# Gated mix of linear attention and a gated MLP: weight sums on another engine, the last chain's sums spread over more units

## The chip, the cores and the metric

The kernel runs on one core of one Trainium2 chip. The time is the device time of one execution in microseconds (us), the median of several executions. TensorE (PE) multiplies; VectorE (DVE), ScalarE (ACT) and GpSimd (POOL) do elementwise work; the queue of SyncE (SP) issues nearly all DMAs, in program order. Each engine works through its own instructions in order and waits on semaphores for the others.

## The reference

For x of 2048 rows and 576 columns the kernel computes, in float32:

```python
g = sigmoid((x * gate_w).sum(-1, keepdims=True))
a = linear_attention(x, wqkv) @ wo          # 32 heads of 18
h = gelu(x @ w_gate) * (x @ w_up)           # 576 -> 4608
b = h @ w_down                              # 4608 -> 576
out = g * a + (1 - g) * b
```

The change touches the MLP alone: the end of the gate and up products, and the whole of `h @ w_down`, called down here.

## The kernel before

Each float32 operand is split into a high part (rounded on ACT) and a low part (the rest, subtracted on DVE or POOL), and a product is three matmuls: high by high, high by low, low by high. Fewer products are made by fast matrix multiplication, which trades products for sums of blocks.

**Gate and up.** A list of *chains* (`CHAINS`), one per block of 256 hidden columns, half of the rows, and gate or up, each of seven products (lines 854 for the matmul). A table `plan`, filled by `put(frame, i, do)`, says what else is issued after step `i` of a frame, so it sets the order on all engines. `weight_sums` (line 373, four subtractions on POOL) prepares the block sums of the next weights. `s_make` (line 1240) makes low parts of the sums of x; for the last third of the rows of x that is on POOL. The chain ends with `extras`: sums of blocks of h that down will need (lines 996 and 999, on DVE, 128 by 512 each), which are stored to DRAM by SP (line 1008), some after loading an earlier block back (line 1014). The last chain's sums cannot be made before it ends, and are made during down, from the list `late`, whose entries `later()` takes off one by one.

**Down.** 26 products (the table `DOWN`), each of three *units* `c` = 0, 1, 2, so 78 units numbered u from 0. A unit is 36 matmuls (line 1377) in four groups of rows t, in two halves. Its operands:

- h: loaded raw from DRAM (line 1210) into one of three raw buffers (a fourth, `e123`, joins when `later()` says so), then `h_make(j)`: high part on ACT (1217 or 1220), low part on DVE (1218 for a negated one, 1221 else), 128 by 1536. There are four places for the result.
- weights: blocks of `w_down` loaded by line 1167 into tiles of 128 by 864. `weight.sums(j)` (line 1178) makes the sums of such blocks that the table names (`made`), `weight.make(j)` the high part on ACT (1183) and the low part on POOL (1184). There are fifteen tiles, and three more once `late` is empty.

At the third unit of a product the results in PSUM are added into the accumulator `acc` by DVE (line 1387, 128 by 288, with the factor 1 - g), once per group of rows and per place in the output where the product counts. Line 1383 copies a result to another set of banks where a later product starts from it. Where the next product goes on in the same banks (a `c` in the table), its first matmul must wait until DVE has read them. That holds for products 0 and 1 (units 0 to 2, then unit 3), and again for product 4, which starts at unit 12 in the banks of product 3.

The main loop of down, which sets the order on every engine:

```python
    for u in range(len(UNITS)):
        unit(u, 0)
        h_make(u + 3)
        w_make(u + 3)
        w_sums(u + 5)
        unit(u, 1)
        if u % 3 != 2:
            later()
        if u in (7, 12, 20):
            acc_load((0, 2, 3)[(7, 12, 20).index(u)])
```

`w_sums(j)` also issues the weight loads up to unit j + 3. `acc_load(i)` loads a quarter of the attention result into `acc`.

Of the kernel before, what the change touches and what calls it, by code (L numbers as in the profile page):

```python
# [114 lines left out]
def tile_gated_mix(ctx, tc, xt, xs, xn, wk, wv, wq, wo, wgu, wdn, cst, out):  # L115
    nc = tc.nc
# [247 lines left out]
    def do(n=1):  # L364
        for _ in range(n):
            todo.popleft()()
            load()

    def weight_sums(raw, out, parts=slice(0, 4)):
        b12, b11, b21, b22 = (raw[:, i] for i in range(4))  # L370
        t1, t2, t3, t4 = (out[:, i] for i in range(4))
        for o, a, b in ((t1, b12, b11), (t2, b22, t1), (t3, b22, b12), (t4, b21, t2))[parts]:
            nc.gpsimd.tensor_tensor(o, a, b, OP.subtract)  # L373
# [93 lines left out]
    for t in range(FIRST, NST):  # L467
# [3 lines left out]
        n, now = DO.get(t, 0), early[0] if t in MAKE else None  # L471
# [251 lines left out]
    class Chunk:  # L723
# [15 lines left out]
        def sums(self):  # L739
            sum_blocks(self.raw, nc.vector)  # L740
# [93 lines left out]
    def f_(i):  # L834
# [181 lines left out]
    def extras(c):  # L1016

        p, n, m = CHAINS[c]
# [3 lines left out]
        s0, s1, s2 = (sx[:, k] for k in range(3))  # L1022
        r0, r1, r2 = mid["u2"], mid["u3"], r_tile
# [23 lines left out]
        def get(k, dst):  # L1047
            return lambda: load_a(g, k, dst)
# [14 lines left out]
        if p == 0:  # L1063
# [5 lines left out]
        f0, f3 = ("a", "d") if n else (f[0], f[3])  # L1069
# [62 lines left out]
    raw_free = deque([0])  # L1132
    vt = [stage[:, i * 864:(i + 1) * 864] for i in range(5)]

    class Weights:
# [34 lines left out]
        def sums(self, j):  # L1170
            m, c = UNITS[j]
            for name, x, op, y in DOWN[m].made:
                dead = [k for k in (x, y) if any(b == j for _, b in self.spans[k, c]) and k != DOWN[m].v
                        and not any(k in (q[1], q[3]) for q in DOWN[m].made[DOWN[m].made.index((name, x, op, y)) + 1:])]
                a, b = self.tile(x, c), self.tile(y, c)
                self.at[name, c] = self.at.pop((dead[0], c)) if dead else self.free.pop(0)
                eng = nc.gpsimd if c == 1 or c == 2 and m % 2 else nc.vector
                eng.tensor_tensor(self.tile(name, c), a, b, OP.add if op == "+" else OP.subtract)

        def make(self, j):  # L1180
# [94 lines left out]
    split_at(2, 6, UP, (5, 6), (3, 4))  # L1275
    put(3, 0, lambda: w_split_raw(2, 3))
    split_at(3, 1, UP, (6, 7))
    put(3, 2, lambda: weight_sums(wraw, tsum))
    split_at(5, 0, GATE, (0, 2))
    split_at(5, 1, GATE, (4, 5))  # L1280
    split_at(5, 3, GATE, (5, 6), (3, 4))
# [23 lines left out]
    late = []  # L1305
    for c in range(len(CHAINS)):
        for (frame, i), does in sorted(extras(c).items()):
            if c < LAST or (frame, i) in ((0, 3), (0, 4)):
                for do in does:
                    put(c + frame, i, do)  # L1310
            elif frame < 0:
                for k, do in enumerate(does):
                    put(LAST + k // 2, (2, 6)[k % 2], do)
            elif (frame, i) == (0, 6):
                late[0] += does
            else:
                late.append(does)
# [43 lines left out]
    def acc_load(i):  # L1361
        for t in range(4):
            nc.sync.dma_start(acc[:, i, :, t], ga_d[4 * i + t].rearrange("p (n c) -> p n c", n=2))

    def unit(u, half):
# [8 lines left out]
        for t in (2 * half, 2 * half + 1):  # L1374
# [9 lines left out]
            for minus, i, j in d.reads:  # L1384
# [3 lines left out]
                if not any((i, j) == r[1:] for x in DOWN[m + 1:] for r in x.reads):  # L1388
                    nc.sync.dma_start(out[st * 128:(st + 1) * 128, j * 288:(j + 1) * 288], o)

    def later():
        if late:
            for do in late.pop(0):
                do()
            if not late:
                raw_free.append(3)
                weight.free.extend((15, 16, 17))

    weight.fetch(7)
    acc_load(1)  # L1400
    w_sums(4)
    for u in range(len(UNITS)):
        unit(u, 0)
        h_make(u + 3)
        w_make(u + 3)
        w_sums(u + 5)
        unit(u, 1)
        if u % 3 != 2:
            later()
        if u in (7, 12, 20):  # L1410
            acc_load((0, 2, 3)[(7, 12, 20).index(u)])
    down.close()
    mlp.close()
    fixed.close()
# [71 lines left out]
```

## Time and profile before

| | |
|---|---|
| median of 3 runs | 1461.57 us (1458.74 to 1464.64) |
| the profiled execution | 1459.33 us, its span 1457.5 us |
| PE busy | 1442.2 us, 99% of the span |
| DVE, ACT, POOL busy | 971.7, 640.7, 827.5 us |
| down (first to last matmul of line 1377) | 1068.28 to 1454.35 us |

The page gives busy times of one execution. PE is nearly always busy, so what a change can bring is read from the places where PE waits; the timeline of PE names these waits in brackets with the releaser, which is the last event that came before and not always the cause.

### The profile page before, as it was taken

To read this page: it belongs to the slowest core of one execution; us is meant where nothing else is said; L and a number is where in the kernel's file an instruction comes from. 1 tells how busy PE (TensorE), PEld (TensorE's weight loads), DVE (VectorE), ACT (ScalarE), POOL (GpSimd) and SP (SyncE) were. 2 spreads that over 40 slices of the span, in tenths; PEclk is the share of its full clock that TensorE was granted. 3 is DMA by queue.
4 is the path that set the end of the run, shared out by engine and by line. 5 is a ranking of instruction groups with operands and counts; after the bars stand their busy time and mean duration, and the time that the engine had idled before them with its cause. 6 is when DMAs were issued, how large, how long until landed. Compare 5 with 4: busy or idle time off the path is not lost. (4 is left out here: it accounts for less than half of the span.)

```text
span 1457.5 us, 21123 instructions
## 1 busy us (share of the span) xinstructions
PE 1442.2 (99%) x8096; PEld 1286.7 (88%) x8096; DVE 971.7 (67%) x1113; ACT 640.7 (44%) x863; POOL 827.5 (57%) x513
## 2 busy tenths in 40 slices
PE   9999999999999999999999999999989899999999
PEld 9999899878888888888888888888889899999999
DVE  7887898443745537465364753647569988799793
ACT  7554656443333443333433334433344454544542
POOL 1674543465554545545445444545157768799895
PEclk9999999999999999999999999999999999999999
DMA  7574486653634436354353543436887896766771
GB/s 258 160 207 137 156 265 192 244 221 122 224 122 140 157 116 217 130 177 141 103 202 130 202 138 114 168 132 224 313 314 282 279 335 203 245 210 228 242 242 49
DMA packets 123925, 282.13 MB, mean 194 GB/s; under 512 B 12008, under 2 KB 39208, under 8 KB 122672
## 3 DMA queue, kind: packets, MB, share of 16 engines
q1 hardware_dynamic: 121232, 275.80, 55.5%
q10 hardware_dynamic: 2592, 4.98, 0.9%
q8 instruction: 63, 1.03, 0.3%
q14 instruction: 38, 0.31, 0.1%
HBM read 182.20 MB, written 98.50 MB: 193 GB/s over the span
## 5 line engine op out<-in xcount | busy, mean ns | idle before, releaser
L854 PE MATMUL bank<-xo,wg 128*128 128x512 f32 x1764 | 415.7, 389 | 1.4 <-POOL xo L1240 0.9
L854 PE MATMUL bank<-xo,wu 128*128 128x512 f32 x1715 | 403.5, 389 | 0.0
L854 PEld LDWEIGHTS bank<-xo,wg 128*128 128x128 f32 x1764 | 330.7, 188 | 70.9 <-POOL xo L1240 1.3
L854 PEld LDWEIGHTS bank<-xo,wu 128*128 128x128 f32 x1715 | 321.8, 188 | 67.2 <-DVE bank L976 0.4
L1377 PE MATMUL bank<-xo 128*128 128x288 f32 x2124 | 289.1, 297 | 8.2 <-ACT xo L1220 4.5
L1377 PEld LDWEIGHTS bank<-xo 128*128 128x128 f32 x2124 | 285.8, 190 | 9.6 <-issue 4.7
L373 POOL TENSOR_TENSOR stage<-stage 128x384 f32<-128x384 f32 x132 | 136.2, 1054 | 166.4 <-DMA stage<-wgu 163.7
L943 ACT ACTIVATE bank<-bank 128x512 f32<-128x512 f32 x139 | 80.9, 582 | 243.1 <-PE bank L854 237.9
L869 POOL TENSOR_TENSOR wg<-stage,wg 128x768 fp32r<-128x768 f32 (+3 forms) x41 | 73.8, 1801 | 127.3 <-ACT wg L868 122.7
L1184 POOL TENSOR_TENSOR xo<-vt,xo 128x864 fp32r<-128x864 f32 x39 | 118.8, 3051 | 34.1 <-ACT xo L1183 33.9
L869 POOL TENSOR_TENSOR wu<-stage,wu 128x768 fp32r<-128x768 f32 (+2 forms) x36 | 74.5, 2071 | 83.5 <-ACT wu L868 79.3
L976 DVE TENSOR_TENSOR bank<-bank,mid 128x512 f32<-128x512 f32 x36 | 25.1, 698 | 143.3 <-ACT mid L971 143.2
L1184 POOL TENSOR_TENSOR xo<-stage,xo 128x864 fp32r<-128x864 f32 x28 | 79.1, 2830 | 49.5 <-ACT xo L1183 49.5
L1377 PE MATMUL bank<-xo,wu 128*128 128x288 f32 x684 | 93.9, 295 | 0.7 <-DVE acc L1387 0.7
L1377 PEld LDWEIGHTS bank<-xo,wu 128*128 128x128 f32 x684 | 91.7, 188 | 1.0 <-issue 0.9
L973 DVE TENSOR_TENSOR f<-bank,mid 128x512 f32<-128x512 f32 x18 | 12.5, 692 | 114.6 <-ACT mid L971 110.4
L971 ACT ACTIVATE mid<-bank 128x512 f32<-128x512 f32 x71 | 42.5, 599 | 101.7 <-PE bank L854 90.3
L781 PEld LDWEIGHTS pair<-kw,p 128*128 128x128 f32 x448 | 60.8, 189 | 1.0
L781 PE MATMUL pair<-kw,p 128*128 128x288 f32 x448 | 61.4, 295 | 0.0
L531 PE MATMUL bank<-xo,qw 128*128 128x512 f32 (+1 forms) x231 | 55.7, 392 | 0.0
L531 PEld LDWEIGHTS bank<-xo,qw 128*128 128x128 f32 (+1 forms) x231 | 41.9, 183 | 10.0
L870 POOL TENSOR_TENSOR wg<-stage,wg 32x384 fp32r<-32x384 f32 (+3 forms) x41 | 48.3, 1179 | 3.2
(262 smaller groups left out, 2199.6 us busy)
## 6 DMA issues: line engine op xcount, KB each, us to landing
wg<-h_d SPq DMA_DIRECT2D x40, 768.0 KB, 4.4
stage<-wgu SPq DMA_DIRECT2D x33, 768.0 KB, 4.9
h_d<-sx SPq DMA_DIRECT2D x72, 256.0 KB, 2.6
xo<-h_d SPq DMA_DIRECT2D x23, 768.0 KB
h_d<-mid SPq DMA_DIRECT2D x63, 256.0 KB, 3.6
h_d<-e SPq DMA_DIRECT2D x63, 256.0 KB, 4.8
vt<-wdn SPq DMA_DIRECT2D x25, 432.0 KB, 5.1
e<-h_d SPq DMA_DIRECT2D x14, 768.0 KB, 4.4
```

The costliest lines, as they stand in the source:

```text
L373: nc.gpsimd.tensor_tensor(o, a, b, OP.subtract)
L531: nc.tensor.matmul(ps[:wa.shape[1]], wa, xa, start=(k == 0), stop=(k == len(ops) - 1), skip_group_check=g == 4)
L781: nc.tensor.matmul(y[:, i, :288], p[:, 5 * a + g], KW[g][:, wl, i * 288:(i + 1) * 288], start=(n == 0), stop=(n == 13))
L854: nc.tensor.matmul(ps, w_, x_, start=start and i == 0, stop=i == 6, skip_group_check=not start)
L869: nc.gpsimd.tensor_tensor(w[:, i, 3:5], src[:, :, 0:2], f32(w[:, i, 0:2]), OP.subtract)
L870: nc.gpsimd.tensor_tensor(w[64:96, i, 2], src[64:96, :, 2], f32(w[64:96, i, 2]), OP.subtract)
L943: nc.scalar.activation(o, src, AF.Copy)
L971: nc.scalar.activation(d_sum, d, AF.Copy)
L973: nc.vector.tensor_tensor(es[3], ps["c"], d_sum, OP.add)
L976: nc.vector.tensor_tensor(d, ps["c"], d_sum, OP.add)
L1184: nc.gpsimd.tensor_tensor(w[:, 1], src, f32(w[:, 0]), OP.subtract)
L1377: nc.tensor.matmul(y, h[:, hl, g, t * 128:(t + 1) * 128], w[:, wl, g * 288:(g + 1) * 288], start=first and c == 0 and n == 0, stop=c == NK ...
```

## The change

Five edits:

1. In the gate and up part, `weight_sums(wraw, tsum)` moves from step 2 to step 4 of frame 3.
2. `weight.sums(j)` for j up to 4 runs on DVE. The third product's and later ones keep their engine. In effect the two sums of unit 4 move from POOL to DVE; those of unit 5 stay on POOL.
3. `w_sums(4)` is called in unit 0, behind `h_make(3)` and `w_make(3)`, not ahead of the loop.
4. The last chain's 18 sums are a list in a new order, each entry with its loads. They were issued in units 0, 1, 3, 4, 6, 7, 9, 10, 12, 13, 15, 16, 18; now in the units of `LATER`, which reach 41 in fact. Three early loads (of x, y and 7 and the like) are placed later. The fourth raw buffer joins at unit 21, not 18; the three weight tiles after unit 41, not 18.
5. The load of quarter 0 of the accumulator is issued at unit 5, not 7.

```diff
+        if not n:
+            return [[get("7", r0), get("6", e[0])],
+                    [do(add, e[1], f[0], e[1]), get("8", r1)],
...
+                    [do(add, f[1], f[1], f[3], "bz")]]
...
-                eng = nc.gpsimd if c == 1 or c == 2 and m % 2 else nc.vector
+                eng = nc.gpsimd if j > 4 and (c == 1 or c == 2 and m % 2) else nc.vector
...
-    put(3, 2, lambda: weight_sums(wraw, tsum))
+    put(3, 4, lambda: weight_sums(wraw, tsum))
...
+    LATER = 3, 4, 7, 9, 12, 15, 18, 21, 24, *range(27, 45, 2)
+
     def later():
         if late:
             for do in late.pop(0):
                 do()
+            if len(late) == 18 - E_FREE:
+                raw_free.append(3)
             if not late:
-                raw_free.append(3)
                 weight.free.extend((15, 16, 17))
...
-    w_sums(4)
     for u in range(len(UNITS)):
         unit(u, 0)
         h_make(u + 3)
         w_make(u + 3)
+        if not u:
+            w_sums(4)
         w_sums(u + 5)
         unit(u, 1)
-        if u % 3 != 2:
+        if u in LATER:
             later()
-        if u in (7, 12, 20):
-            acc_load((0, 2, 3)[(7, 12, 20).index(u)])
+        if u in (5, 12, 20):
+            acc_load((0, 2, 3)[(5, 12, 20).index(u)])
```

Line numbers of the changed kernel are 16 to 20 higher: 1178, 1184, 1218, 1221, 1240, 1387 became 1198, 1204, 1238, 1241, 1260, 1403.

On POOL in frame 3 of gate and up, before (-) and now (+); `xo` is the second operand set, `stage` the raw weights and their sums:

```order
-L1240 TENSOR_TENSOR xo_3263<-f,xo_3263 32x4x256
-L373 TENSOR_TENSOR stage<-stage 128x384 x4
-L1240 TENSOR_TENSOR xo_3263<-f,xo_3263 32x4x256
+L1260 TENSOR_TENSOR xo_3263<-f,xo_3263 32x4x256 x2
+L373 TENSOR_TENSOR stage<-stage 128x384 x4
```

The four weight sums have moved behind the second low part of x.

On POOL where down begins, before; the first row is the low parts of the weights of units 0 to 2, the single 1184 is unit 3's, and `vt` and `stage` hold weight blocks:

```order
L1184 TENSOR_TENSOR xo<-stage,xo 128x864 x3
L1178 TENSOR_TENSOR vt_8789<-vt_8788,vt_8789 128x864
L1178 TENSOR_TENSOR stage<-vt_8789,stage 128x864
L1184 TENSOR_TENSOR xo<-stage,xo 128x864
L1178 TENSOR_TENSOR vt_8791<-vt_8790,vt_8791 128x864
L1178 TENSOR_TENSOR stage<-vt_8791,stage 128x864
L1184 TENSOR_TENSOR xo<-stage,xo 128x864 x3
```

The same place now:

```order
L1204 TENSOR_TENSOR xo<-stage,xo 128x864 x4
L1198 TENSOR_TENSOR vt_8788<-vt_8787,vt_8788 128x864
L1198 TENSOR_TENSOR stage<-vt_8788,stage 128x864
L1204 TENSOR_TENSOR xo<-stage,xo 128x864 x3
L1204 TENSOR_TENSOR xo<-vt_8785,xo 128x864
```

Unit 3's low part no longer has unit 4's two sums ahead of it, and unit 4's low part has two sums ahead of it instead of four.

On DVE at the same place, before; 1218 are the low parts of h of units 3 and 4, 996 and 999 the last chain's sums, 1387 the first reads of product 0:

```order
L1178 TENSOR_TENSOR stage<-stage 128x864 x2
L1218 SCALAR_TENSOR_TENSOR xo<-xo 128x1536
L996 TENSOR_TENSOR e_3256<-f,e_3256 128x512
L996 TENSOR_TENSOR e_3256<-e_3256,mid 128x512
L1218 SCALAR_TENSOR_TENSOR xo<-wg,xo 128x1536
L999 TENSOR_TENSOR mid<-mid,f 128x512
L996 TENSOR_TENSOR mid<-f,mid 128x512
L1387 SCALAR_TENSOR_TENSOR acc<-bank,probe,acc 128x288 x2
```

And now:

```order
L1198 TENSOR_TENSOR stage<-stage 128x864 x2
L1238 SCALAR_TENSOR_TENSOR xo<-xo 128x1536
L1198 TENSOR_TENSOR vt_8786<-vt_8785,vt_8786 128x864
L1198 TENSOR_TENSOR stage<-vt_8786,stage 128x864
L1238 SCALAR_TENSOR_TENSOR xo<-wg,xo 128x1536
L1403 SCALAR_TENSOR_TENSOR acc<-bank,probe,acc 128x288 x2
```

Four of the last chain's sums have left the place ahead of the first reads, and unit 4's two weight sums stand there.

On DVE ahead of the reads of product 3, which unit 12 waits for, before:

```order
L1221 TENSOR_TENSOR xo<-xo 128x1536
L1178 TENSOR_TENSOR vt_8794<-vt_8794,stage 128x864
L996 TENSOR_TENSOR mid<-mid,sx 128x512
L996 TENSOR_TENSOR f<-f 128x512
L1221 TENSOR_TENSOR xo<-wg,xo 128x1536
L1178 TENSOR_TENSOR stage<-vt_8795,vt_8796 128x864
L999 TENSOR_TENSOR mid<-mid,f 128x512
L996 TENSOR_TENSOR sx<-f,sx 128x512
L1387 SCALAR_TENSOR_TENSOR acc<-bank,probe,acc 128x288 x2
```

And now:

```order
L1241 TENSOR_TENSOR xo<-xo 128x1536
L1198 TENSOR_TENSOR vt_8791<-vt_8791,stage 128x864
L996 TENSOR_TENSOR mid<-f,mid 128x512
L1241 TENSOR_TENSOR xo<-wg,xo 128x1536
L1198 TENSOR_TENSOR stage<-vt_8792,vt_8793 128x864
L1403 SCALAR_TENSOR_TENSOR acc<-bank,probe,acc 128x288 x2
```

Of four sums of the last chain between the low part of unit 12 and those reads one is left.

More of the change, by code (lines that the diff above doesn't have):

```diff
@@ L1068, in extras @@
                     (1, 6): [do(add, s2, e[2], s1, "b3")]}
-        f0, f3 = ("a", "d") if n else (f[0], f[3])
+        if not n:
+            return [[get("7", r0), get("6", e[0])],
+                    [do(add, e[1], f[0], e[1]), get("8", r1)],
+                    [do(add, e[1], e[1], r0, "a7b7"), get("9", r2)],
+                    [do(sub, e[0], e[0], f[0], "a6b6"), get("x", e[3])],
+                    [do(add, r0, f[0], r0, "a7b6")],
+                    [do(sub, r1, f[2], r1, "a8b8"), do(sub, e[2], f[2], e[2])],
+                    [do(add, e[2], e[2], r2, "a9b9"), get("4", r0)],
+                    [do(add, s1, f[0], f[1], "bx"), get("5", r1)],
+                    [do(add, e[3], e[3], s1, "axbx")],
+                    [do(sub, r0, r0, f[3], "a4b4"), get("y", e[0])],
+                    [],
+                    [do(add, s2, s1, f[3], "by"), hold("b8", f[2])],
+                    [do(add, s1, r2, f[2], "a9b8")],
+                    [do(sub, r2, s2, r2, "a9by")],
+                    [do(add, s0, f[3], s0)],
+                    [do(add, s0, s0, r1, "a5b5")],
+                    [do(add, r1, f[3], r1, "a5b4")],
+                    [do(sub, e[0], f[0], e[0], "ayb6")],
+                    [do(add, f[1], f[1], f[3], "bz")]]
+        f0, f3 = "a", "d"
         return {(-1, 5): [get("7", r0), get("x", r1), get("y", r2)],
@@ L1304, in tile_gated_mix @@
     kept = [(0, es[1], (2, 4), (LAST, 1)), (1, sx[:, 0], (2, 4), (LAST, 1)), (2, es[2], (2, 6), (LAST, 3))]
-    late = []
-    for c in range(len(CHAINS)):
+    for c in range(1, LAST):
         for (frame, i), does in sorted(extras(c).items()):
[L1308 to L1317, printed above, removed]
+            for do in does:
+                put(c + frame, i, do)
+    late = extras(LAST)
+    for do in late.pop(0):
+        put(LAST, 4, do)
+    E_FREE = late.index([])
+    late.pop(E_FREE)
     for k, src, (frame, i), (back, j) in kept:
```

## The prediction

> **What bounds the kernel now.** I read the page first. Its first part says that PE is the bound, so only places where PE waits or runs slowly can give time back.
>
> ```profile
> PE 1442.2 (99%) x8096; PEld 1286.7 (88%) x8096; DVE 971.7 (67%) x1113; ACT 640.7 (44%) x863; POOL 827.5 (57%) x513
> ```
>
> Next the timeline of PE alone, for rows with a bracket (start, duration, count, idle time before and its releaser), and the chain that ended last for the pace of an undisturbed stretch.
>
> ```profile
> 313.61 2.11 PE L854 MATMUL bank<-xo,wg 128*128 128x512 f32 x8 [0.89 <-POOL xo L1240]
> 1068.28 9.71 PE L1377 MATMUL bank<-xo 128*128 128x288 f32 x72
> 1083.14 0.63 PE L1377 MATMUL bank<-xo 128*128 128x288 f32 x3 [0.38 <-DVE acc L1387]
> 1084.51 5.15 PE L1377 MATMUL bank<-xo 128*128 128x288 f32 x36 [0.74 <-POOL xo L1184]
> 1092.20 10.91 PE L1377 MATMUL bank<-xo 128*128 128x288 f32 x69 [2.54 <-POOL xo L1184]
> 1136.12 11.29 PE L1377 MATMUL bank<-xo 128*128 128x288 f32 x72 [4.52 <-ACT xo L1220]
> 1167.22 5.08 PE L1377 MATMUL bank<-xo,wu 128*128 128x288 f32 x36 [0.73 <-DVE acc L1387]
> 1313.27 141.08 PE bank L1377 x1062
> ```
>
> The undisturbed pace is 141.08/1062 = 0.1328 us for one matmul, 4.78 for a unit of 36. Down has 78 units, 2808 matmuls, and at this pace needs 373.0 us. It takes from 1068.28 to 1454.35 (1313.27 + 141.08), 386.1. So down loses 13.1 us. Five waits hold 8.9 of it (0.38 + 0.74 + 2.54 + 4.52 + 0.73). Two stretches behind a wait are slow: 72 matmuls take 11.29 us where the first 72 took 9.71 (1.6 more), and 69 take 10.91 where 9.71 x 69/72 = 9.3 would do (1.6 more). The last 1.0 is spread over the restarts. The slow stretches are seen in PE's clock, asked for in windows of 2 us (columns: busy, granted clock, DMA share, GB/s):
>
> ```profile
> 1084.50:1087.00 2.50, 2.49 (x18) 1.00 0.40 153
> 1092.20:1094.20 2.00, 2.00 (x9) 0.58 0.03 8
> 1138.10:1140.10 2.00, 2.00 (x10) 0.50 0.90 342
> ```
>
> After 2.54 and 4.52 us of waiting the clock is at half; after 0.38 and 0.74 it is full. Above 2 us a wait therefore costs some 1.6 more than it lasts. The Trainium skill ("TensorE: Matmul & The Clock Gate", section "HAM oscillation — how this bites in real kernels") warns of gaps over about 3.4 us. By that page the 2.54 us wait would have cost nothing in clock, and this change would be worth 1.6 less, an estimate of 1450.1 where the sum below gives 1448.5. The trace does not agree: it shows a clock of 0.58 behind that wait, and the measurement decides.
>
> **Part 1, the sums moved in gate and up.** The first row above waits for a low part of x on POOL. These are POOL's rows there, and ACT's that feeds it:
>
> ```profile
> 304.25 1.06 ACT L1239 ACTIVATE xo<-f 128x1024 fp32r<-128x1024 f32 x1 [1.13 <-DMA f<-xsum_d]
> 307.06 4.05 POOL L373 TENSOR_TENSOR stage<-stage 128x384 f32<-128x384 f32 x4
> 311.18 2.37 POOL L1240 TENSOR_TENSOR xo<-f,xo 32x1024 fp32r<-32x1024 f32 x1
> ```
>
> The low part could start at 305.3 but stands behind 4.05 us of weight sums. In the new order it goes first, ends near 309.5 instead of 313.55, and the 0.89 us wait goes. The sums then end near 313.5, and their readers come in frame 5, two chains later. Gain 0.9, little doubt.
>
> **Parts 2 and 3, unit 4's sums to DVE.** Here are the rows where down begins, SP, POOL and DVE:
>
> ```profile
> 1063.08 0.32 SPq L1014 DMA_DIRECT2D e<-h_d  x1
> 1065.89 0.32 SPq L1014 DMA_DIRECT2D r<-ha_d8y  x1
> 1068.47 1.92 SPq L1167 DMA_DIRECT2D vt<-wdn  x4
> 1076.50 3.06 POOL L1178 TENSOR_TENSOR vt<-vt,vt 128x864 f32<-128x864 f32 x1 [14.99 <-DMA vt<-wdn]
> 1079.63 2.38 POOL L1178 TENSOR_TENSOR stage<-vt,stage 128x864 f32<-128x864 f32 x1
> 1081.97 2.49 POOL L1184 TENSOR_TENSOR xo<-stage,xo 128x864 fp32r<-128x864 f32 x1
> 1084.41 3.64 POOL L1178 TENSOR_TENSOR vt<-vt,vt 128x864 f32<-128x864 f32 x1
> 1090.14 7.53 POOL L1184 TENSOR_TENSOR xo<-stage,xo 128x864 fp32r<-128x864 f32 x3
> 1072.89 1.75 DVE L1218 SCALAR_TENSOR_TENSOR xo<-xo 128x1536 fp32r<-128x1536 f32 x1
> 1077.55 2.55 DVE L999 TENSOR_TENSOR mid<-mid,f 128x512 f32<-128x512 f32 x1
> 1080.03 2.54 DVE L996 TENSOR_TENSOR mid<-f,mid 128x512 f32<-128x512 f32 x1
> 1082.48 0.93 DVE L1387 SCALAR_TENSOR_TENSOR acc<-bank,probe,acc 128x288 f32<-128x288 f32 x2
> ```
>
> POOL waits to 1076.50 for unit 4's weight blocks with unit 3's low part queued behind, which so ends at 1084.46: the 0.74 wait. Unit 5's sums then hold unit 4's low part until 1092.2: the 2.54 wait. In the new order unit 3's low part runs once its sums (1072.9) and their high part are there, near 1074.6 to 1076.6. Unit 4's low part then has only unit 5's sums ahead. Both POOL waits go.
>
> DVE is where a price comes in. The rows show that POOL and DVE take turns: POOL's first sum ends at 1079.56 and the DVE sum requested at 1077.55 ends 0.54 later; POOL's second ends at 1082.01 and DVE's next 0.56 later. So a turn costs POOL about 1.95, DVE 0.55 for 512 elements, 1.75 for the 1536 of a low part, and about 1.05 for the 864 of a weight sum (row of 1131.48 below). On DVE the two sums of unit 4, then the low part of h of unit 4, now stand ahead of the first reads of product 0, for which unit 3 waits, due at 1068.28 + 3 x 4.78 = 1082.6. If unit 5's blocks have landed by 1077.6, turns run: POOL to 1076.6, DVE 1077.6, POOL 1079.6, DVE 1080.6, POOL 1082.5, DVE's low part 1084.2, first read 1084.7. Unit 3 then starts near 1084.9, some 2 us late, against 0.5 before. If they land later, DVE does its two sums in a row and the reads end before 1082.6: no wait. Three loads of 256 KB (the first and last are the first two SP rows) no longer precede the blocks. At this rate
>
> ```profile
> GB/s 374 290 166 239 359 336 383 405 404 405 407 386 361 410 386 390 400 315 311 350 346 354 411 405 385 380 350 390 440 386 424 429 395 398 200 51 99 217 405 217
> ```
>
> of about 390 (the DMA view from 1056 to 1090) that is 2 us earlier: unit 4's blocks near 1074.5, unit 5's two near 1076.7 (0.88 MB, 2.2 us later). I therefore take the late case, a new wait of 2.0, bounds 0 and 2.0 + 1.6 if the clock falls. I leave the clock alone because 2.0 lies between waits that kept it (1.1 in all) and one that lost it (2.54), and so keep 1.6 as doubt.
>
> **Part 4, the last chain's sums.** The 4.52 us wait at 1136.12 names ACT, but unit 12 goes on in product 3's banks, and DVE's first read there began at 1135.46 and took half of 0.93: it ended 0.2 before PE started, as at 1083.14. DVE was late:
>
> ```profile
> 1114.79 2.54 DVE L996 TENSOR_TENSOR e<-f,e 128x512 f32<-128x512 f32 x1
> 1117.26 2.55 DVE L996 TENSOR_TENSOR sx<-f 128x512 f32<-128x512 f32 x1
> 1131.48 1.04 DVE L1178 TENSOR_TENSOR stage<-vt,vt 128x864 f32<-128x864 f32 x1
> 1132.45 0.68 DVE L999 TENSOR_TENSOR mid<-mid,f 128x512 f32<-128x512 f32 x1
> 1133.05 2.49 DVE L996 TENSOR_TENSOR sx<-f,sx 128x512 f32<-128x512 f32 x1
> 1135.46 0.93 DVE L1387 SCALAR_TENSOR_TENSOR acc<-bank,probe,acc 128x288 f32<-128x288 f32 x2
> ```
>
> The last two sums alone are 3.2 us, and one of the pair at 1114.79 goes too, 2.5 more. Together 5.7, above 4.52. The wait and its slow stretch, 4.5 + 1.6, go. The 0.73 wait at 1167.22 is of the same kind; the sum ahead of it,
>
> ```profile
> 1164.11 2.54 DVE L999 TENSOR_TENSOR r<-sx,r 128x512 f32<-128x512 f32 x1
> 1166.00:1313.00 147.00, 146.27 (x1102) 145.92 (x1100) 120.75 (x82) 72.72 (x66) 118.54 (x41) 1.00 0.73 249
> ```
>
> moves to unit 31. The second row is the window behind that wait (busy: PE, PEld, DVE, ACT, POOL): DVE is idle for 26 us of 147. Eleven sums now fall there or at its edge, where one did: ten more at 0.68 to 2.55 are 7 to 26 us. At a mean of 1.6 they fit. I put 0 on it; the upper bound is one wait as at 1092.20, 2.5 + 1.6.
>
> **Part 5, one accumulator load two units earlier**, plus later loads of blocks: the same bytes. Its four DMAs stand ahead of unit 5's h load on SP instead of unit 7's; nothing reads the quarter before unit 11. Cost 0.
>
> **The sum.** Gained: 0.9 + 13.1 = 14.0; lost: 2.0; net 12.0. The profiled execution took 1459.33, 2.2 under the median of 1461.57. 1459.33 - 12.0 = 1447.3; from the median 1449.6. I predict between them, 1448.5.
>
> **The rivals.**
>
> *One more late read.* DVE and POOL share turns, so a sum moved to a busy place makes another read late, between units 18 and 42, with the clock behind it: 4.1 to 6 us back, 1452.5 to 1454.5. For it: DVE at 82% in that window. Against: no wait at all in 1172 to 1454 before. Chance 0.18.
>
> *The DVE backlog stays.* The change does not do what it says at unit 12: the two weight sums put on DVE and the entries kept at units 3, 4, 7 and 9 hold the queue as before, and 4.5 + 1.6 remain, 1454.6. Against: unit 6 is emptied, and unit 10. Chance 0.10.
>
> *Slower, through the weight tiles.* With fifteen tiles until unit 41, loads at units 19 to 21 and 25 to 27 go into a tile given up one unit before. SP then waits for that unit's low part on POOL, with the load of h behind it.
>
> ```profile
> wg<-h_d SPq DMA_DIRECT2D x40, 768.0 KB, 4.4
> ```
>
> Such a load (KB, us to landing) is issued three units, 14.3 us, ahead of its unit; with 4.4 for landing and some 5 for the split about 5 us are to spare. It decides from a hold of more than 5 us; if all six times cost 2.5 + 1.6, that is 24.6, 1473. Three already give the gain back. Against: POOL's low part mostly ends within the unit. Chance 0.06.
>
> **Chances and range.** My forecast has 0.63 (own range 1445 to 1451: no wait at unit 3 and a profile-like run below, 2.0 + 1.6 above), the remaining 0.03 for what I have not thought of. Faster by over 0.5% means under 1454.3, and 0.5% is about what a measurement of this kernel can tell from no change: the forecast and most of the first rival, 0.78. Within: the second rival and some of the others, 0.15. Slower: 0.07. The range 1445 to 1456 takes in the forecast and the first two rivals.
>
> **What would show it.** Right: no bracket at PE's frame 3; at unit 3 one wait released by DVE's read; no wait for a low part of weights at units 3 and 4; PE at full clock from 1085 to 1175; the stretch of down near 375 us. Wrong: a bracket of over 2 us released by DVE's read at units 12, 18, 24, 27, 33 or 36, where a product goes on in banks just read, or an SP wait for POOL with ACT waiting for a load of h.

## The result, and the profile after

| | before | after |
|---|---|---|
| median | 1462.28 us (1458.74 to 1464.64, 6 runs) | 1452.80 us (1451.79 to 1452.96, 6 runs) |
| profiled execution, its span | 1459.33, 1457.5 | 1452.77, 1451.0 |
| PE, DVE, POOL busy | 1442.2, 971.7, 827.5 | 1437.3, 989.0, 823.6 |
| down, first to last matmul | 386.1 | 380.2 |

The changed kernel takes 0.9936 of the time, interval [0.9923, 0.9949]: faster by 9.5 us between the medians and by 6.6 between the two profiled executions. The profiled execution of before was one of its faster ones; what follows explains the 6.6. The 2.9 between 9.5 and 6.6 lie in executions of which there is no trace, and stay unexplained. The prediction was 1448.5, so the gain is real and some 4 us smaller than forecast.

Here are the rows with a bracket of the changed kernel's PE timeline, from the end of gate and up on (start, duration, instructions, idle time before and its releaser):

```profile
1065.88 1.88 PE L854 MATMUL bank<-xo,xo 128*128 128x512 f32 x7 [0.90 <-DVE bank L976]
1083.84 2.60 PE L1393 MATMUL bank<-xo 128*128 128x288 f32 x18 [1.84 <-DVE acc L1403]
1087.28 12.18 PE L1393 MATMUL bank<-xo 128*128 128x288 f32 x90 [0.83 <-DVE acc L1403]
1157.35 2.61 PE L1393 MATMUL bank<-xo,wu 128*128 128x288 f32 x18 [0.58 <-DVE acc L1403]
1160.78 2.65 PE L1393 MATMUL bank<-xo,wu 128*128 128x288 f32 x18 [0.83 <-DVE acc L1403]
1190.61 7.43 PE L1393 MATMUL bank<-xo 128*128 128x288 f32 x54 [0.83 <-DVE acc L1403]
1231.76 2.62 PE L1393 MATMUL bank<-xo 128*128 128x288 f32 x18 [0.32 <-DVE acc L1403]
1235.20 2.63 PE L1393 MATMUL bank<-xo 128*128 128x288 f32 x18 [0.81 <-DVE acc L1403]
1293.14 2.64 PE L1393 MATMUL bank<-xo 128*128 128x288 f32 x18 [0.72 <-DVE acc L1403]
```

Down starts at 1067.60, so with 36 matmuls to a unit these are unit 3 (its two halves), unit 18 (both), 24 (second half), 33 (both) and 45 (second half). Each goes on in banks that DVE has to read first. Gone are the wait for the low part of x in frame 3, both waits for POOL at units 3 and 4, and the wait at unit 12 with its half clock; the clock is 1.00 behind every row. New are the wait of 1.84 at unit 3, which was forecast as 2.0, and seven smaller ones. The waits' view sums the eight of down (us in total, times, longest):

```profile
PE bank L1393 <- DVE acc L1403: 6.8, 8, 1.8
```

So the account of down closes: it loses 380.2 - 373.0 = 7.2 us to its pace without waits, against 13.1 before, and 6.8 of that stands in this one row.

Why a second half waits 0.83 is seen on DVE and POOL at unit 3:

```profile
1076.90 2.83 DVE L1198 TENSOR_TENSOR stage<-vt,stage 128x864 f32<-128x864 f32 x1
1078.89 2.76 POOL L1198 TENSOR_TENSOR stage<-vt,stage 128x864 f32<-128x864 f32 x1
1079.65 3.62 DVE L1238 SCALAR_TENSOR_TENSOR xo<-wg,xo 128x1536 fp32r<-128x1536 f32 x1
1081.61 10.62 POOL L1204 TENSOR_TENSOR xo<-stage,xo 128x864 fp32r<-128x864 f32 x3
1083.19 0.93 DVE L1403 SCALAR_TENSOR_TENSOR acc<-bank,probe,acc 128x288 f32<-128x288 f32 x2
1084.04 2.75 DVE L1238 SCALAR_TENSOR_TENSOR xo<-wg,xo 128x1536 fp32r<-128x1536 f32 x1
1086.72 0.93 DVE L1403 SCALAR_TENSOR_TENSOR acc<-bank,probe,acc 128x288 f32<-128x288 f32 x2
```

Between the two pairs of reads DVE makes a low part of h. Alone that is 1.75 us; in turns with POOL, which makes three low parts of weights at the same time, it is 2.75. The reads of the second half then start 3.53 us behind those of the first, while PE needs 2.60 for half a unit. The 0.93 between is about the wait of 0.83. The first of the two low parts took 3.62, so 1.87 more than alone: about one whole turn of POOL, which the prediction put at 1.95.

Unit 33 shows the waits that the moved sums make. DVE again:

```profile
1228.22 2.55 DVE L999 TENSOR_TENSOR r<-sx,r 128x512 f32<-128x512 f32 x1
1230.68 1.78 DVE L1403 SCALAR_TENSOR_TENSOR acc<-bank,gate,acc 128x288 f32<-128x288 f32 x4
```

The sum of 2.55 us stands directly ahead of the reads that PE waits for. At unit 45 the moved sum is further off: the last one ended near 1279.2 and the first read of the pair began at 1289.04, but DVE was never idle between, so the delay stayed in its queue. The window that the prediction used for room, now:

```profile
1166.00:1313.00 147.00, 144.32 (x1084) 143.24 (x1083) 138.74 (x87) 70.41 (x64) 119.45 (x41) 1.00 0.74 260
```

DVE (third pair) is busy 138.74 of 147 us, 18.0 more than before, inside the 7 to 26 that the prediction gave for the ten sums. In total they fit, with 8 us to spare; by place they do not. (Time in which an instruction of DVE stands behind POOL counts as busy here.)

### The profile page after: what moved, and what is told of

The parts are those of the page before. It is cut to its first block, busy times and chain, and to the rows that moved or that the text cites. A ratio compares the mean times of both kernels' runs of the same rounds, so it can differ in the third digit from the quotient of the medians.

```text
span 1451.0 us, 21113 instructions
## 1 busy us (share of the span) xinstructions
PE 1437.3 (99%) x8096; PEld 1281.7 (88%) x8096; DVE 989.0 (68%) x1115; ACT 640.8 (44%) x863; POOL 823.6 (57%) x511
## 5 line engine op out<-in xcount | busy, mean ns | idle before, releaser
L1393 PE MATMUL bank<-xo 128*128 128x288 f32 x2124 | 285.5, 295 | 5.4 <-DVE acc L1403 5.4
L1393 PEld LDWEIGHTS bank<-xo 128*128 128x128 f32 x2124 | 282.0, 188 | 6.9 <-DVE acc L1403 4.1
L1204 POOL TENSOR_TENSOR xo<-vt,xo 128x864 fp32r<-128x864 f32 x42 | 124.2, 2965 | 27.9 <-ACT xo L1203 26.5
L1204 POOL TENSOR_TENSOR xo<-stage,xo 128x864 fp32r<-128x864 f32 x32 | 96.0, 3005 | 66.2 <-ACT xo L1203 66.2
L1241 DVE TENSOR_TENSOR xo<-wg,xo 128x1536 fp32r<-128x1536 f32 x18 | 48.9, 2718 | 5.2 <-ACT xo L1240 5.2
```

The costliest lines, as they stand in the source:

```text
L1204: nc.gpsimd.tensor_tensor(w[:, 1], src, f32(w[:, 0]), OP.subtract)
L1241: nc.vector.tensor_tensor(h[:, 1], raw, f32(h[:, 0]), OP.subtract)
L1393: nc.tensor.matmul(y, h[:, hl, g, t * 128:(t + 1) * 128], w[:, wl, g * 288:(g + 1) * 288], start=first and c == 0 and n == 0, stop=c == NK ...
```

## The experiments

Every kernel was timed against before on the same chip. The chips differ from kernel to kernel (the medians of before lie between 1460.9 and 1462.3), so differences of about 1 us between two medians below mean little, and the rows of the traces decide. Theory A, with which the experiments start: each of the changed kernel's waits is a late read of DVE, late by the one or two instructions directly ahead of it that take turns with POOL; so it goes when that instruction goes elsewhere. Its rival at first is that the weight tiles and loads that part 4 also moves cause them. Letters in the expectations are explained where they come up.

### What part 4 is worth

**late_sums_out**: the changed kernel without eleven sums of the last chain; their loads and stores stay.

```diff
-                    [do(add, s1, f[0], f[1], "bx"), get("5", r1)],
+                    [stored(add, s1, f[0], f[1], "bx"), get("5", r1)],
...
-                    [do(add, f[1], f[1], f[3], "bz")]]
+                    [stored(add, f[1], f[1], f[3], "bz")]]
```

> Leaves out the eleven sums of the last chain that the changed kernel makes from unit 18 on (their loads and stores stay, so the stored blocks hold other data). Theory A, VectorE's queue: these sums are what makes the reads at units 24, 33 and 45 late, so the waits at 1190.61 (0.83), 1231.76 and 1235.20 (0.32, 0.81) and 1293.14 (0.72) go, 2.7 us, and those at units 3 and 18 (1.84, 0.83, 0.58, 0.83) stay: about 1450.1. Theory B, the three weight tiles and the fourth raw buffer that come later hold loads and so the engines: the waits at 24, 33 and 45 stay and the time is 1452.8 within 1.

Measured 1449.92 us (1448.12 to 1450.74), 0.9924 [0.9909, 0.9939]. The waits of PE in its trace:

```profile
PE bank L1396 <- DVE acc L1406: 4.0, 4, 1.7
```

The four that stay are those of units 3 and 18 (1.74, 0.82, 0.62, 0.82). Those at units 24, 33 and 45, 2.7 us in all, went with the sums, and the median fell by 2.9 (the intervals of the two ratios overlap; down itself is 2.4 shorter in the traces). So the sums themselves cost that, and not the weight tiles or the queue of loads, which were as they were. The waits at unit 18 are not from these eleven sums.

**old_late_order**: before, with parts 1, 2, 3 and 5, that is, the change without part 4.

```diff
-                eng = nc.gpsimd if c == 1 or c == 2 and m % 2 else nc.vector
+                eng = nc.gpsimd if j > 4 and (c == 1 or c == 2 and m % 2) else nc.vector
...
-    w_sums(4)
...
+        if not u:
+            w_sums(4)
```

> The kernel before with all edits but the last chain's sums, which stay in their old units and order (0 to 18). Theory A: the waits at units 12 (4.5 and 1.6 of half clock) and 18 (0.7) come back, those at 24, 33 and 45 go (2.7), and at unit 3 four old sums stand ahead of the reads beside unit 4's two, so the read there is later by up to 5 and the clock falls: 1452.8 + 6.8 - 1.4 - 2.7 + 3 to 6 = 1458.5 to 1461.5. Theory B (what matters at unit 12 is not these sums): unit 12 keeps running without a wait, 1451 to 1455.

Measured 1467.27 us (1466.89 to 1467.9), 1.0045 [1.003, 1.006]: slower than before by 5.6 (its median beside it was 1461.7), and 14.5 slower than the whole change. PE, and DVE ahead of the first of the two rows:

```profile
1092.15 17.02 PE L1377 MATMUL bank<-xo 128*128 128x288 f32 x108 [9.76 <-DVE acc L1387]
1145.78 11.17 PE L1377 MATMUL bank<-xo 128*128 128x288 f32 x72 [7.97 <-DVE acc L1387]
```

```profile
1075.69 1.50 DVE L1178 TENSOR_TENSOR vt<-vt,vt 128x864 f32<-128x864 f32 x1 [1.33 <-DMA vt<-wdn]
1077.29 1.06 DVE L1178 TENSOR_TENSOR stage<-vt,stage 128x864 f32<-128x864 f32 x1
1078.26 2.56 DVE L996 TENSOR_TENSOR e<-f,e 128x512 f32<-128x512 f32 x1
1080.85 2.42 DVE L996 TENSOR_TENSOR e<-e,mid 128x512 f32<-128x512 f32 x1
1083.19 3.57 DVE L1218 SCALAR_TENSOR_TENSOR xo<-wg,xo 128x1536 fp32r<-128x1536 f32 x1
1086.69 2.48 DVE L999 TENSOR_TENSOR mid<-mid,f 128x512 f32<-128x512 f32 x1
1089.10 2.49 DVE L996 TENSOR_TENSOR mid<-f,mid 128x512 f32<-128x512 f32 x1
1091.50 0.93 DVE L1387 SCALAR_TENSOR_TENSOR acc<-bank,probe,acc 128x288 f32<-128x288 f32 x2
```

The four old sums, 2.42 to 2.56 us each in turns, and unit 4's two weight sums all stand ahead of the first reads. Unit 3 waits 9.76 us and unit 12 as well, 7.97, each more than theory A had expected (up to 5 later, and 4.5), so the time lies well above its 1458.5 to 1461.5. Parts 2 and 3 by themselves move the late work from POOL to DVE and lose; part 4 makes the place for them.

### Parts 1, 2 and 3

**gate_up_sums_old**: part 1 undone.

```diff
-    put(3, 4, lambda: weight_sums(wraw, tsum))
+    put(3, 2, lambda: weight_sums(wraw, tsum))
```

> The changed kernel with part 1 undone: the four weight sums of frame 3 back at step 2. If the prediction's term is right, PE waits 0.9 us at frame 3 for the low part of x, with full clock behind it: 1452.8 + 0.9 = 1453.7. Rival: POOL has time there in some executions and the term is nothing, 1452.8.

Measured 1454.63 us (1453.95 to 1455.75), 0.9954 [0.9942, 0.9967]. PE, and the POOL rows that it waits for:

```profile
314.51 2.14 PE L854 MATMUL bank<-xo,wg 128*128 128x512 f32 x8 [1.06 <-POOL xo L1260]
```

```profile
307.95 4.07 POOL L373 TENSOR_TENSOR stage<-stage 128x384 f32<-128x384 f32 x4
312.09 2.37 POOL L1260 TENSOR_TENSOR xo<-f,xo 32x1024 fp32r<-32x1024 f32 x1
```

The wait is back, 1.06 where the prediction had 0.89, behind the same four sums. The median is 1.8 above that of the changed kernel, but the intervals of the two ratios overlap; the row settles it.

**unit4_sums_on_pool**: parts 2 and 3 undone, part 4 kept.

```diff
-                eng = nc.gpsimd if j > 4 and (c == 1 or c == 2 and m % 2) else nc.vector
+                eng = nc.gpsimd if c == 1 or c == 2 and m % 2 else nc.vector
...
+    w_sums(4)
...
-        if not u:
-            w_sums(4)
```

> The changed kernel with unit 4's weight sums back on POOL and ahead of the loop. Theory A: the two waits for POOL's low parts come back (1.0 at unit 3, 2.9 at unit 4, 1.6 of half clock behind it), the reads of product 0 are on time, so 1.84 and 0.83 go: 1452.8 + 5.5 - 2.7 = 1455.6. Rival, the last chain's sums alone had made POOL late (by taking turns), and with them away POOL is in time: 1450 to 1451.

Measured 1455.95 us (1455.79 to 1456.82), 0.9965 [0.9952, 0.9977]. PE's rows up to unit 12:

```profile
1086.45 3.04 PE L1393 MATMUL bank<-xo 128*128 128x288 f32 x21 [1.62 <-DVE acc L1403]
1089.92 9.41 PE L1393 MATMUL bank<-xo 128*128 128x288 f32 x69 [0.43 <-POOL xo L1204]
1129.27 2.62 PE L1393 MATMUL bank<-xo 128*128 128x288 f32 x18 [1.29 <-DVE acc L1403]
1132.68 7.43 PE L1393 MATMUL bank<-xo 128*128 128x288 f32 x54 [0.80 <-DVE acc L1403]
```

The time is within 0.4 us of what was expected, by other waits than expected. Two waits named POOL, of 1.0 and 2.9 with half clock, had been looked for; one of 0.43 is there. But the 1.62, at the second half of unit 3, names DVE and comes from POOL as well. These rows are of POOL, ACT and DVE in turn:

```profile
1074.73 2.06 POOL L1198 TENSOR_TENSOR vt<-vt,vt 128x864 f32<-128x864 f32 x1 [12.47 <-DMA vt<-wdn]
1080.35 0.93 ACT L1203 ACTIVATE xo<-stage 128x864 fp32r<-128x864 f32 x1 [5.22 <-POOL stage L1198]
1082.69 3.27 DVE L1238 SCALAR_TENSOR_TENSOR xo<-wg,xo 128x1536 fp32r<-128x1536 f32 x1 [2.05 <-ACT xo L1237]
1085.89 0.93 DVE L1403 SCALAR_TENSOR_TENSOR acc<-bank,probe,acc 128x288 f32<-128x288 f32 x2
```

ACT waits for POOL's second sum of unit 4 with the high part of h queued behind, DVE waits for that, and the reads stand behind its low part. So undoing parts 2 and 3 costs 2.05 us at units 3 and 4 (1.62 + 0.43), where before lost 3.66 (0.38 + 0.74 + 2.54) and 1.6 by the clock. The rest is gone with part 4: among other things unit 4's blocks land earlier, so that POOL's first sum starts 6.7 us after the first matmul of down, and not 8.2. The changed kernel waits 2.67 at unit 3, no less than 2.05. What parts 2 and 3 save, with part 4 in place, shows at unit 12, which waits 2.09 here and not at all there; the medians differ by 3.2.

### Trying to take the remaining waits away

**unit5_sums_later**: both sums of unit 5, on POOL, one unit later, so that the first reads of product 0 find DVE without those turns.

```diff
-        w_sums(u + 5)
+        for j in {0: (), 1: (5, 6)}.get(u, (u + 5,)):
+            w_sums(j)
```

> The changed kernel with unit 5's weight sums issued in unit 1, behind unit 4's low part, instead of in unit 0. Theory A, turns: POOL's two sums of unit 5 no longer take turns with VectorE's sums of unit 4 and low part ahead of the first reads, so VectorE reaches them near 1080 and both waits of unit 3 (1.84 and 0.83) go: 1450.2. Rival, the first reads wait for their accumulator tile or for unit 4's blocks: the 1.84 stays, 1452 to 1453. If unit 5's low part is then late, a new POOL wait at unit 5 of up to 1 us.

Measured 1454.17 us (1453.72 to 1454.88), 0.9955 [0.994, 0.997]. The first row of PE with a bracket in down is now this:

```profile
1126.26 11.36 PE L1393 MATMUL bank<-xo 128*128 128x288 f32 x72 [2.38 <-DVE acc L1403]
```

Both waits at unit 3 (1.84 and 0.83) are gone, as theory A says. In their place unit 12 waits 2.38 with a slow stretch behind it: 72 matmuls take 11.36 us, not 9.7. The median is 1.4 above that of the changed kernel, outside both ranges expected; the intervals of the two ratios overlap, so at best nothing was won.

**low_behind_reads**: at the end of a product whose banks the next goes on in, the low part of h goes behind the second reads.

```diff
+        tight = u % 3 == 2 and u // 3 + 1 < len(DOWN) and DOWN[u // 3 + 1].goes_on and DOWN[u // 3].reads
+        if not tight:
+            h_make(u + 3)
...
         unit(u, 1)
+        if tight:
+            h_make(u + 3)
```

> The changed kernel; in the last unit of a product whose banks the next one goes on in, the high and low parts of h for three units on are issued behind the second half's reads, not between the two halves' reads. Theory A (the second wait of each pair comes from the low part that takes a turn of 2.75 between the reads): the second-half waits at units 3, 18, 24, 33, 45 (0.83, 0.83, 0.83, 0.81, 0.72, 4.0 in all) go, the first ones (1.84, 0.58, 0.32) stay: 1448.8. Rival, the second reads are late by the same backlog as the first, whatever stands between: the pairs stay or move to the first half, 1452 to 1454.

Measured 1453.8 us (1451.39 to 1456.1), 0.9953 [0.9937, 0.997], where 1448.8 was expected. PE, three of its five rows with a bracket in down:

```profile
1083.22 14.48 PE L1393 MATMUL bank<-xo 128*128 128x288 f32 x108 [1.74 <-DVE acc L1403]
1127.62 9.74 PE L1393 MATMUL bank<-xo 128*128 128x288 f32 x72 [1.44 <-DVE acc L1403]
1301.96 9.77 PE L1393 MATMUL bank<-xo 128*128 128x288 f32 x72 [1.69 <-DVE acc L1403]
```

The five waits of a second half are gone, 4.0 us in all, and so are those at units 18 and 33; new ones stand at units 12, 36, 48 and 72 (1.44, 0.34, 1.69, 0.50), which the changed kernel did not have. This shows what made a second half wait, and that most of what is won there is lost elsewhere: the waits of down are 5.7 in all, not 6.8. The trace is of the fastest of the executions, 1451.39; what the slower ones lost is not shown.

**later_behind_reads**: the sums of the last chain from unit 14 on, in units that follow such reads.

```diff
-    LATER = 3, 4, 7, 9, 12, 15, 18, 21, 24, *range(27, 45, 2)
+    LATER = 3, 4, 7, 9, 12, *range(14, 48, 3)
```

> The changed kernel with the last chain's sums from the sixth entry on issued in units 14, 17, 20 up to 47, each just behind the reads of a product, instead of 15, 18, 21, 24, 27, 29 to 41. Theory A: two units more lie between a sum and the next reads, so the waits at units 18, 24, 33 (0.58, 0.83, 0.83, 0.32, 0.81) shrink to under 1 in all; one at 45 or 48 may grow, as the sums now reach unit 47: 1450 to 1451. Rival, the share of VectorE and POOL is full there and any place is as bad: 1452 to 1453.5.

Measured 1454.5 us (1453.58 to 1455.8), 0.9956 [0.9939, 0.9973]: no gain. The two waits at unit 33 went, those at unit 18 stayed (0.58 and 0.80), and unit 48 waits instead, 1.22 and then 0.81:

```profile
1306.30 2.62 PE L1393 MATMUL bank<-xo 128*128 128x288 f32 x18 [1.22 <-ACT xo L1237]
```

**unit5_later_acc_at_3**: unit5_sums_later with the accumulator load of part 5 at unit 3. Theory C in this expectation is that the load, at unit 5, makes unit 12 late.

```diff
-        if u in (5, 12, 20):
-            acc_load((0, 2, 3)[(5, 12, 20).index(u)])
+        if u in (3, 12, 20):
+            acc_load((0, 2, 3)[(3, 12, 20).index(u)])
```

> Unit 5's sums in unit 1 as in the run before, and quarter 0 of the accumulator loaded at unit 3 instead of unit 5. Theory C (in that run the wait of 2.38 at unit 12 came from loads: the accumulator's 1.2 MB stood ahead of unit 12's h load, in a stretch where the DMA engines are full): the wait at unit 12 goes, with its half clock, and the waits of unit 3 stay away: 1452.8 - 2.7 = 1450.1. Rival, VectorE's own queue (the sums at units 7 and 9) makes the reads at unit 11 late once PE runs ahead: the wait of 2 to 2.5 and the half clock stay, 1453.5 to 1454.5.

Measured 1455.82 us (1453.62 to 1458.58), 0.9967 [0.9956, 0.9978].

```profile
1130.47 11.32 PE L1393 MATMUL bank<-xo 128*128 128x288 f32 x72 [4.09 <-DVE acc L1403]
```

The wait at unit 12 grew from 2.38 to 4.09. That theory fell; the time is above the range of its rival too.

**all_three**: unit5_later_acc_at_3 with the edits of low_behind_reads and later_behind_reads.

> All three edits of this call together on the changed kernel. Theory A with C: down has no wait but bits: 1452.8 - 6.8 = 1446 to 1447. Rival (each wait removed lets PE run into the next limit, loads or the shared turns): 1449 to 1451.

Measured 1457.67 us (1456.27 to 1460.37), 0.9977 [0.9967, 0.9987], the worst of this group. PE:

```profile
1129.24 12.38 PE L1393 MATMUL bank<-xo 128*128 128x288 f32 x72 [5.01 <-DVE acc L1403]
1305.89 11.22 PE L1393 MATMUL bank<-xo 128*128 128x288 f32 x72 [2.07 <-DVE acc L1403]
```

Both expectations were far too low. All small waits up to unit 12 are gone, and PE pays for them there at once, 5.01 us and the clock. Theory A describes the waits at unit 3 and in the second halves rightly, but the waits are not independent: without them PE comes sooner to the next late read.

### What holds unit 12

From here on theory C is another one: the loads of h, three raw buffers in a stretch where the DMA engines are full, make DVE's low parts late. Theory D: DVE's queue itself is full between units 6 and 11, in turns with POOL.

**unit5_later_third_of_h**: unit5_sums_later with two thirds of the bytes of eight loads of h left out.

```diff
-            nc.sync.dma_start(raw_at[raw_of[j]], h_d[c][:, m])
+            k = 1 if 6 <= j < 14 else 3
+            nc.sync.dma_start(raw_at[raw_of[j]][:, :k], h_d[c][:, m][:, :k])
```

> unit5_sums_later with two thirds of the bytes left out of the loads of h of units 6 to 13 (the kernel then computes with old values there). In unit5_sums_later unit 12 waits 2.38 us for DVE's reads and its clock is half behind it, and ACT waits 13.3 us for loads of h between 1095 and 1130. Theory C (those loads, at 400 GB/s, make DVE's low parts and so the reads late): ACT's waits for the DMA fall to under 4, the wait at unit 12 to under 0.7, full clock: 1454.2 - 2.4 - 1.6 = about 1450. Theory D (DVE's own queue, with turns against POOL, is full there whatever arrives when): the wait stays at 1.5 to 2.4 us, 1452.5 to 1454.

Measured 1453.45 us (1452.01 to 1454.27), 0.9943 [0.993, 0.9957]. PE, then a window between units 6 and 11 (busy PE, PEld, DVE, ACT, POOL; clock, DMA share, GB/s):

```profile
1127.99 2.61 PE L1394 MATMUL bank<-xo 128*128 128x288 f32 x18 [3.35 <-DVE acc L1404]
```

```profile
1094.00:1126.00 32.00, 30.64 (x233) 30.41 (x231) 32.00 (x18) 16.76 (x17) 24.43 (x9) 1.00 0.80 284
```

The DMA engines moved 284 GB/s in that window, not 336 as in unit5_sums_later, and the wait did not shrink: 3.35. Theory C fell, in so far as it is about bytes. DVE is busy for all 32 us, as theory D says, though the wait is longer than its 1.5 to 2.4. ACT still waited 13.4 us for loads of h (1094 to 1130), and the waits of SP point to a reason (window 1060 to 1130):

```profile
SPq L1231 <- DVE xo L1242: 13.8, 5, 5.1
```

In this kernel a load is only issued when DVE has given up a raw buffer, so a late DVE makes late loads however small they are.

**unit5_later_sum9_at_11**: one sum of 2.54 us taken from ahead of those reads.

```diff
-    LATER = 3, 4, 7, 9, 12, 15, 18, 21, 24, *range(27, 45, 2)
+    LATER = 3, 4, 7, 11, 12, 15, 18, 21, 24, *range(27, 45, 2)
```

> unit5_sums_later with one sum of the last chain (2.54 us, it runs at 1120.51, ahead of product 3's reads) issued in unit 11, behind those reads, not in unit 9; every load as it was. Theory D: the first read starts 2.5 us earlier, near 1123.1, so unit 12 starts on its own time; wait under 0.5, full clock, about 1450.2 against 1452.8 of the changed kernel. Theory C: DVE only idles longer for the loads of h; the wait stays above 1.5, 1452.5 to 1454.

Measured 1455.77 us (1453.02 to 1456.43), 0.9956 [0.9942, 0.9971]; unit 12 waits 2.52 with half clock. DVE, a little ahead of the place:

```profile
1117.80 1.76 DVE L1241 TENSOR_TENSOR xo<-xo 128x1536 fp32r<-128x1536 f32 x1 [2.31 <-ACT xo L1240]
...
1122.31 3.60 DVE L1241 TENSOR_TENSOR xo<-wg,xo 128x1536 fp32r<-128x1536 f32 x1
```

The 2.54 us that were taken away came back: DVE waits 2.31 for ACT, which waits for a load of h, where it had waited 1.39, and a low part that now meets POOL takes 3.60, not 1.75. That is 2.8 more. Theory D, as worded, fell here too.

**unit5_later_h6_first**: theory E. In unit5_sums_later ACT stands at the high part of unit 5's weights, which need POOL's late sums, and DVE is idle for 5.56 us behind it. Two steps on ACT are exchanged.

```diff
-        h_make(u + 3)
-        w_make(u + 3)
+        if u != 3:
+            h_make(u + 3)
+        if u != 2:
+            w_make(u + 3)
...
         unit(u, 1)
+        if u == 2:
+            h_make(6)
+            w_make(5)
```

> unit5_sums_later with two steps on ACT exchanged: the high part of h of unit 6 ahead of the high part of the weights of unit 5. Theory E: in unit5_sums_later ACT stands 6.88 us before the latter, which waits for POOL's late sums of unit 5, and DVE's low part of h of unit 6 stands 5.56 us behind that; from there DVE has no idle time worth naming until it is late at unit 11's reads. With the exchange DVE's hole of 5.56 shrinks to under 2, the first read of unit 11 comes 3 to 4 us earlier, near 1122, the wait at unit 12 (2.38 with half clock) goes: about 1450.2, with at most 1 us lost at unit 5, whose low part of weights ends near its start. Theories C and D (loads, or DVE's own work there): the hole closes but the reads of unit 11 come near 1125.5 to 1127 all the same, the wait stays over 1.5, 1452.5 to 1455.

Measured 1453.16 us (1451.78 to 1454.78), 0.9948 [0.9934, 0.9961]. PE, and the same window:

```profile
1129.25 11.27 PE L1393 MATMUL bank<-xo 128*128 128x288 f32 x72 [3.20 <-DVE acc L1403]
```

```profile
1094.00:1126.00 32.00, 32.00 (x242) 31.81 (x240) 32.00 (x17) 17.18 (x18) 25.59 (x10) 1.00 0.87 322
```

DVE's hole closed from 5.56 to 2.63, and the wait is 3.20 all the same: theory E fell. POOL, which in unit5_sums_later is idle for 2.22 and 3.40 us between 1101 and 1111, now works without a break from 1090.65 to 1107.83, and both go in turns: five DVE instructions between 1092.79 and 1109.44 that are 1.75 and 0.68 alone take 2.56 to 3.62 (four of the five did before), and the two behind them 2.90 and 2.55, not 1.04 and 0.68. That is 5.6 more.

Put side by side, counted from the first matmul of down, with all waits of PE up to unit 12:

| kernel | waits to unit 12 | clock behind | first read of unit 11 |
|---|---|---|---|
| the changed kernel | 2.67 | full | 58.6 |
| unit4_sums_on_pool | 4.14 | full | 60.6 |
| low_behind_reads | 3.18 | full | 59.9 |
| unit5_sums_later | 2.38 | half | 58.9 |
| unit5_later_sum9_at_11 | 2.52 | half | 59.0 |
| unit5_later_h6_first | 3.20 | half | 60.0 |
| unit5_later_third_of_h | 4.16 | full | 59.8 |
| unit5_later_acc_at_3 | 4.09 | half | 60.6 |
| all_three | 5.01 | half | 61.5 |

The reads come 58.6 to 61.5 us after the start of down, whatever is moved ahead of them. PE without waits would be at unit 12 at 12 x 4.78 = 57.4. So in all nine orders PE waits 2.4 to 5.0 us up to there; the changed kernel waits near the least, and at unit 3, in two pieces behind which the clock stayed full. One reading fits these rows, a ring of which each link was seen: DVE gives up a raw buffer, SP issues the load, ACT makes the high part in a place that PE has finished with, DVE the low part in turns with POOL. Shortening one link (bytes, a sum, a hole) lengthened another. Which link is the longest depends on when PE comes: between 1094 and 1130 ACT waits 7.1 us for PE to give up places and 6.7 for loads of h in the changed kernel, and 4.5 and 13.3 in unit5_sums_later, where PE is not held up at unit 3. That the ring sets the time is argued and not shown, as no run shortened it as a whole; fewer POOL sums in units 3 to 9 and a fourth raw buffer there were not tried. No version measured is clearly faster than the changed kernel; late_sums_out, which is below it, leaves work out.

## Why the prediction was right, and where it was not

- **Bound by PE's waits.** Right: the rows of waits account for 6.8 of the 7.2 us that down still loses. Of the change from 13.1 to 7.2, the waits are 2.1, and the two slow stretches behind waits that are gone 3.2.
- **Part 1.** Right: the wait is gone with the edit and back without it, 0.89 predicted, 1.06 measured.
- **Parts 2 and 3, gains.** The POOL waits went, but the step that gave parts 2 and 3 the whole credit failed. With them undone and part 4 kept, units 3 and 4 wait 2.05 at full clock, where before lost 3.66 and 1.6 by the clock: the greater part went with part 4. With them done unit 3 waits 2.67, and what they bring shows at unit 12 (2.09). Without part 4 they cost time: old_late_order is 5.6 above before.
- **Parts 2 and 3, the new wait.** Predicted 2.0 at unit 3 with the clock left alone, measured 1.84 with full clock. The turns were counted rightly there, and that the clock held was a guess, between a wait that kept it and one that lost it, which came out. What I missed is the second half: the low part of h between the two pairs of reads takes its turns as well, and that costs 0.83 more.
- **Part 4, gains.** Right at unit 12: the wait and its slow stretch are gone, and without part 4 unit 12 waits 7.97. Wrong at unit 18: of the 0.73 nothing was gained, it waits 0.58 + 0.83 now, and not for the eleven later sums, since late_sums_out waits there too.
- **Part 4, the window.** This is the step that failed: "At a mean of 1.6 they fit. I put 0 on it". The room was estimated as a sum over 147 us, and the sum was right (18.0 more of 26 idle), but a wait is decided by what DVE's queue holds ahead of each read. The six waits of units 18 to 45 cost 4.09. That this is near the upper bound of 4.1 is luck: the bound was one wait of 2.5 with 1.6 of slow clock behind it. 2.7 of the 4.09 go when the sums are left out (late_sums_out); the 1.4 at unit 18 do not. They were absent when the low part stood behind the reads (low_behind_reads), where PE also came 0.5 later to unit 18, so that run shows the cause of the 0.83 better than that of the 0.58.
- **Part 5.** Cost 0 was not contradicted, nor shown, as no run undoes part 5 alone. In unit5_later_acc_at_3, with the load two units earlier still, the wait at unit 12 was longer, not shorter.
- **The sum.** 12.0 of gain were forecast from the profiled execution, and 6.6 came: 0.83 at unit 3 and 4.09 in the window, less 0.16 at unit 3, some 0.4 spread over the restarts in down, which the sum had put at nothing, and 0.2 ahead of down (it starts 0.7 sooner, not 0.9) make up the 5.4 between.
- **The rivals.** My likeliest case had 1445 to 1451 and the median is 1452.8. The rival "one more late read", 1452.5 to 1454.5 at 0.18, is the nearest to what came: late reads between units 18 and 45, but six short ones with full clock, not one with the clock behind it. The backlog at unit 12 and the weight tiles did not come. So the forecast missed its own range; the median lies in the whole range because that took in this rival. None of the signs of being wrong came (no wait is over 2 us), but two of the signs of being right did not come either: unit 3 waits twice, and down takes 380.2, not near 375.

## What to carry to other kernels

Where two engines share turns, room for moved work is not read from an average over a stretch: look at each read that PE waits for, and price what stands ahead of it in its engine's queue since that queue was last idle, in turns. Undo the parts of a change one by one: here two parts lose over 5 us without a third and win some 3 with it, and much of the credit for two waits that went belonged to that third part. A wait that names one engine can come from another: here a read of DVE was late through ACT by sums on POOL. When small waits are left that each have a plain cause, add up what PE waits up to the next fixed point; if every reordering only moves that total, look for a common limit behind it.

## What the hardware did that I had not expected

The clock does not follow the length of a wait alone, as the prediction had put it ("above 2 us"). Waits of 1.62 to 1.84 us kept it; 2.07, 2.38, 2.52, 3.20, 4.09 and 5.01 lost it (72 matmuls in 11.2 to 12.4 us, not 9.7); and yet the 3.35 of unit5_later_third_of_h kept it. PE's clock behind that one and behind the 2.38 of unit5_sums_later:

```profile
1128.00:1130.00 2.00, 2.00 (x15) 2.00 (x16) 2.00 (x2) 0.46 (x1) 2.00 (x2) 1.00 0.32 132
```

```profile
1126.00:1128.00 2.00, 1.74 (x8) 1.77 (x9) 2.00 (x3) 0.17 (x2) 1.92 (x1) 0.59 1.02 391
```

The Trainium skill ("TensorE: Matmul & The Clock Gate", "Part 1: The HAM clock gate (the "warmup" mystery)") says that the activity is watched in a window that runs freely. The same gap could then fall differently on that window, which would allow both rows; these runs do not show the window, so it stays a possible reason. The page puts the idle time that lowers the clock at some 3.4 us, and that does not agree with a clock lost after 2.07.

The price of turns is large: on DVE a sum of 512 elements from two operands in SBUF is 0.68 us alone and up to 2.56 beside POOL, a low part of 1536 elements 1.75 alone and up to 3.62, while the reads from PSUM stay at 0.93 for two in every row shown. The Trainium skill ("GPSIMD Engine Reference", "Specifications") says that GpSimd shares its SBUF interfaces with VectorE and names VectorE instructions with two SBUF inputs among those that contend; the rows agree, and the reads have one of their two tensors in PSUM.
